# Inputs laid out on the host in the order of the loads, in a kernel of attention, dense gated layer and expert layer

## The chip, the cores and the metric

One core of one Trainium2 chip runs the whole program once. The metric is the device time of that core in microseconds, as the median of repeated executions; lower is better. The arrays that the kernel is given may be laid out on the host before the launch (a transposition or a reordering by numpy), and that takes no device time.

## The reference

Three layers follow each other, on 2304 tokens of width 512.

```python
scores = scale * np.matmul(q, k.transpose(0, 1, 3, 2))      # q, k, v: 4 x 8 x 576 x 64
ret = scores * Dmat[None, :, :, :]                          # gamma_h ** (i - j) for j <= i
x = np.matmul(ret, v)                                       # -> 2304 x 512

xn = x / rms * rms_g
g = xn @ w_gate                                             # 512 x 1536, float64
x = (g * sigmoid(g) * (xn @ w_val)) @ w_out                 # 1536 x 512, float64

e_idx = np.argmax(x @ w_gate2, axis=1)                      # one of 8 experts for a token
h = np.maximum(x[mask] @ w1[e], 0.0)                        # 512 x 1024
out[mask] = gate_w[mask, None] * eom[mask, e, None] * (h @ w2[e])
```

The weights of the dense layer are float64 on the device too: the kernel reads them as 64-bit integers and makes a high and a low float16 part of each. A product of two split numbers takes three matmuls (high by high, high by low, low by high).

## The kernel before, in words

The tokens are 18 tiles of 128 (`TILES`, L67), in groups (`GROUPS`, L70); group 0 holds tiles 0 to 3, one for each batch entry. For a tile, attention is loaded (`l`), split or transposed (`s`), scored (`c`), put out and normed (`o`), and its recurrent state updated (`z`). Then the dense layer runs over 12 slices of 128 hidden columns: `moe_h` (L828) makes a slice of the hidden activations, `moe_out` (L859) multiplies it by the output weights. At the end come routing and eight experts.

Group 0 is the opening. Its weights arrive in 18 pieces of 1 MB (`load_piece`, L806): piece i below 12 is gate and val of slice i, the other six are two slices of w_out each. `conv_piece` (L817) decodes a piece: `decode` (L784) puts a float64 together as a float32 (an operation on ScalarE, one on VectorE, and for each half a copy into the only PSUM buffer `du` and a VectorE operation out of it), ScalarE rounds it to `gv_h` or `wo_h`, and GpSimd subtracts for `gv_l` or `wo_l`. The raw pieces stand in `fst`, a pool of four buffers.

The first four tiles (`FIRST`, L76) need no state. Their q and k are loaded in rows of 64 numbers for each head (`att_load`, L586), and `split_first` (L603) transposes them on TensorE, eight transposes a tile, into PSUM tiles `tp`, from which ScalarE copies to `tr`. `scores_first` (L618) multiplies in float32, VectorE multiplies by the decay matrix `dmat` into `pp`, and `att_out` (L725) multiplies by v. Tile 2's loads borrow the buffer of tag `r` (`IN_R`).

The order of work is made by a planner (`Plan`, L236). Every operation is recorded with what it reads and writes, and `schedule` (L349) gives each engine a fixed list: at each planned moment an engine takes the ready operation with the lowest due time, which is the position of the first TensorE group that depends on it. A tile's buffers are taken in the recorded order (`_track`, L300), so an operation that first uses a buffer goes ahead of the one that first uses the next buffer of the same tag. `START` (L86) lists the opening's steps in the order in which they are recorded: `d` loads a piece, `k` decodes it, `f` makes `dmat` and `gain`, `h` is `moe_h`, `y` is `moe_out`, `e` clears a table in memory by GpSimd, `m` loads the router's weights. While TensorE has nothing to do in the plan and the first `y` hasn't begun, `fill` (L416) adds a matmul on a constant tile, `busy`, of 256 columns. All loads except those of tables are issued by SyncE (SP) on one queue. `_cost` (L322) has the planner's estimates.

Later tiles load q, k, v in the same short rows (L596). The experts' weights come in slabs of 1 MB (`exp_slab`, L1028) in rows of 2 KB.

Of the kernel before, what the change touches and what calls it, by code (L numbers as in the profile page):

```python
# [88 lines left out]
l4 o3 s4 y1-2-3 d7 k8 d14 k6 c4 d9 y1-0-1 k7 h3-4-3-4 k14 d15 h4-5-0-3 y3-1-2 y3-2-3 h0-2-3-4 k9 d11 e4 h6-7-3-4
h5-6-0-3 z3 d10 y2-0-3 l5 h7-8-0-3 z2 l6 y4-0-2 y5-0-3 d17 h5-6-3-4 k15 o4 z4 k10 m e2 s5 h2-3-3-4 y4-2-3 h6-7-0-3  # L90
y6-0-1 k11 y7-0-2 e8 h8-9-0-3 h4-5-3-4 h8-11-3-4 c5 y6-2-3 y7-2-3 d16 s6 h11-12-0-3 k16 e1 y6-1-2 e6 o5 c6 y8-0-3
k17 h9-11-0-3 o6 z6 e7 e5 y9-0-3 y10-0-1 y10-1-3 y11-0-3 e3 h7-8-3-4 z5 h11-12-3-4 e9
# [406 lines left out]
def body(tc, q, k, v, w_gate, w_val, w_out, rms_g, wg2, wog2, w1, w2, const, decay, empty, out):  # L499
# [169 lines left out]
    def att_scores(t):  # L669
# [358 lines left out]
    def exp_slab(slab, e, after=()):  # L1028
# [3 lines left out]
        def load():  # L1032
            w, at = (w1, slice(512 * slab, 512 * slab + 512)) if slab < 2 else (w2, slice(512 * slab - 1024, 512 * slab - 512))
            one = w[e] if isinstance(e, int) else w[bass.ds(e.result if isinstance(e, Op) else e, 1)].rearrange(
                "o d f -> (o d) f"
            )
            src = one[:, at] if slab < 2 else one[at, :]
            return nc.sync.dma_start(out=real(st), in_=src.rearrange("(k p) f -> p k f", p=P))
# [393 lines left out]
    def start():  # L1432

        for step in START.split():
# [173 lines left out]
```

## Time and profile before

| | us |
|---|---|
| median of 3 runs | 750.03 (749.82 to 750.12) |
| the profiled execution | 752.39 |
| its span | 750.6 |

| engine | busy, us | share of the span |
|---|---|---|
| TensorE, matmuls (PE) | 729.6 | 97% |
| TensorE, weight loads (PEld) | 495.2 | 66% |
| VectorE (DVE) | 432.9 | 58% |
| ScalarE (ACT) | 349.7 | 47% |
| GpSimd (POOL) | 282.1 | 38% |

The busy time of TensorE includes the matmuls on the constant tile. SP's instructions are DMA issues and count as no busy time. A row of the timeline gives start, length, engine, line, operation, output and inputs, and in brackets how long the engine was idle before it and what released it. The line is nearly always L226, the helper that records an operation, so that tile names tell operations apart. The DMA share of a stretch can be above 1, as packets of one engine overlap.

### The profile page before, as it was taken

To read this page: it belongs to the slowest core of one execution; us is meant where nothing else is said; L and a number is where in the kernel's file an instruction comes from. 1 tells how busy PE (TensorE), PEld (TensorE's weight loads), DVE (VectorE), ACT (ScalarE), POOL (GpSimd) and SP (SyncE) were. 2 spreads that over 40 slices of the span, in tenths; PEclk is the share of its full clock that TensorE was granted. 3 is DMA by queue.
4 is the path that set the end of the run, shared out by engine and by line. 5 is a ranking of instruction groups with operands and counts; after the bars stand their busy time and mean duration, and the time that the engine had idled before them with its cause. 6 is when DMAs were issued, how large, how long until landed. Compare 5 with 4: busy or idle time off the path is not lost. (4 is left out here: it accounts for less than half of the span.)

```text
span 750.6 us, 15489 instructions
## 1 busy us (share of the span) xinstructions
PE 729.6 (97%) x6163; PEld 495.2 (66%) x6163; DVE 432.9 (58%) x881; ACT 349.7 (47%) x665; POOL 282.1 (38%) x303
## 2 busy tenths in 40 slices
PE   9999999999899999999999999999999999999994
PEld 7986757656565656556655555677876677778751
DVE  3769898656662476157543626342565777666441
ACT  2789888533432264134422325222334666565450
POOL 2585789743541352215321311131103053313442
PEclk9999999999999999999999999999999999999998
DMA  9969989593670283435432143210089898899731
GB/s 237 255 195 240 271 195 266 116 203 62 132 146 18 61 164 74 73 43 117 82 57 43 58 108 132 43 58 15 15 253 263 258 290 220 264 268 238 186 98 38
DMA packets 212812, 109.84 MB, mean 146 GB/s; under 512 B 179891, under 2 KB 192211, under 8 KB 212594
## 3 DMA queue, kind: packets, MB, share of 16 engines
q1 hardware_dynamic: 209042, 96.30, 54.5%
q0 software_dynamic: 3696, 12.54, 5.2%
q8 instruction: 49, 0.80, 0.5%
q14 instruction: 25, 0.20, 0.1%
HBM read 70.02 MB, written 14.00 MB: 112 GB/s over the span
## 5 line engine op out<-in xcount | busy, mean ns | idle before, releaser
L226 PEld LDWEIGHTS <-gv_h 128*128 128x128 f16 x1440 | 133.3, 98 | 71.9 <-issue 6.0
L288 POOL TENSOR_TENSOR ul<-th,uh 128x384 f16<-128x384 f32 (+2 forms) x77 | 66.8, 868 | 209.1 <-ACT uh L226 207.9
L226 PE MATMUL hg<-xt,gv_h 128*128 128x384 f16 (+2 forms) x624 | 134.6, 305 | 1.9 <-DVE th L226 1.6
L226 PE MATMUL hv<-xt,gv_h 128*128 128x384 f16 (+2 forms) x624 | 135.9, 308 | 0.3 <-DVE th L226 0.3
L226 PEld LDWEIGHTS <-eh 128*128 128x128 f16 x1024 | 97.2, 98 | 30.0
L226 DVE SCALAR_TENSOR_TENSOR th<-th,hg 128x384 f32<-128x384 f32 (+2 forms) x90 | 42.3, 470 | 110.6 <-ACT th L226 110.5
L226 PE MATMUL eh<-ex,eh 128*128 128x288 f16 (+7 forms) x576 | 104.7, 284 | 0.0
L226 PE MATMUL hv<-xt,gv_l 128*128 128x384 f16 (+2 forms) x312 | 94.6, 307 | 0.0
L226 PE MATMUL hg<-xt,gv_l 128*128 128x384 f16 (+2 forms) x312 | 94.1, 305 | 0.0
L226 PEld LDWEIGHTS <-gv_l 128*128 128x128 f16 x720 | 70.6, 98 | 30.7 <-issue 0.7
L226 DVE SCALAR_TENSOR_TENSOR el<-st,eh 128x1024 f16<-128x1024 f32 x64 | 81.8, 1305 | 13.1 <-ACT eh L288 12.0
L226 ACT ACTIVATE uh<-th 128x384 f16<-128x384 f32 (+2 forms) x78 | 37.5, 481 | 97.3 <-DVE th L226 97.2
L226 ACT ACTIVATE th<-hg 128x384 f32<-128x384 f32 (+2 forms) x90 | 38.2, 424 | 93.2 <-PE hg L226 91.9
L226 PE MATMUL eh<-ex,el 128*128 128x288 f16 (+7 forms) x288 | 78.9, 284 | 0.0
L226 PE MATMUL o<-wo_h,ul 128*128 128x512 f16 x204 | 77.3, 379 | 0.0
L226 PE MATMUL o<-wo_h,uh 128*128 128x512 f16 x204 | 77.3, 379 | 0.0
L226 PE MATMUL o<-wo_l,uh 128*128 128x512 f16 x204 | 77.3, 379 | 0.0
L288 ACT ACTIVATE eh<-st 128x1024 f16<-128x1024 f32 x64 | 64.8, 1051 | 4.6 <-DMA st<-in_moe_w 4.6
L226 PE MATMUL ea<-hh,eh 128*128 128x288 f16 (+5 forms) x224 | 64.9, 290 | 0.0
L226 PE MATMUL ea<-hh,el 128*128 128x288 f16 (+5 forms) x224 | 64.9, 290 | 0.0
L226 PE MATMUL ea<-hl,eh 128*128 128x288 f16 (+5 forms) x224 | 64.9, 290 | 0.0
L226 DVE SCALAR_TENSOR_TENSOR th<-th,hv 128x384 f32<-128x384 f32 (+2 forms) x90 | 42.4, 471 | 32.1 <-PE hv L226 30.0
(210 smaller groups left out, 1223.3 us busy)
## 6 DMA issues: line engine op xcount, KB each, us to landing
st<-in_moe_w SPq DMA_DIRECT2D x32, 1024.0 KB
st<-in_moe_w_gate SPq DMA_DIRECT2D x12, 512.0 KB
st<-in_moe_w_val SPq DMA_DIRECT2D x12, 512.0 KB
st<-in_moe_w_out SPq DMA_DIRECT2D x12, 512.0 KB
kf<-in_k SPq DMA_DIRECT2D x15, 256.0 KB
qf<-in_q SPq DMA_DIRECT2D x15, 256.0 KB
vf<-in_v SPq DMA_DIRECT2D x15, 256.0 KB
xs<-in_empty POOLq DMA_DIRECT2D x7, 385.5 KB, 5.8
```

Of the source, the lines that this page charges most:

```text
L226: return call(*map(real, args), **{a: real(b) for a, b in kw.items()})
L288: return getattr(engine, method)(*map(real, args), **{a: real(b) for a, b in kw.items()})
```

## The change

The host transposes and reorders the inputs (`laid_out`), so that each load reads one long row for each partition: q, k and v of a token in rows of 2 KB, a piece of the dense weights in rows of 8 KB by one DMA, a slab of an expert in rows of 8 KB, the router's two tables in one load. For the first four tiles, q and k come transposed as one array `qk_t` (4 KB rows); the TensorE transposes and their copies go, k in rows is still loaded for the state, and q in rows no longer. The pool of raw pieces has five buffers for four, the score tile `pp` two for one; the scores of tiles 0 and 1 and the tables of step `f` use the PSUM pool `pso` in place of `pst`. The planner counts 330 GB/s for every plain load, also for those under 300 KB, and 3.3 us for a slab in place of 3.4. `START` is another list. The scratch for software-made DMA descriptors is set to 4096 bytes.

```diff
 START = """
-l0 d1 f l1 s0 c0 k1 d0 k0 s1 l2 o0 c1 o1 s2 h0-1-0-2 d12 d3 z0 c2 h1-2-0-1 d2 o2 d5 k3 h1-2-1-2 h3-4-0-2 k12
-h3-4-2-3 h0-1-2-3 l3 z1 y0-0-3 s3 c3 d13 k2 h1-2-2-3 d4 e0 h2-3-0-1 y1-1-2 k5 d8 k13 d6 h2-3-1-2 h2-3-2-3 y3-0-1 k4
...
+l2 l1 l0 s1 f d1 s0 s2 c0 o0 k1 d0 z0 d12 c1 d3 o1 k0 h0-1-0-2 d2 z1 k3 c2 h1-2-0-1 h1-2-1-2 o2 z2 h3-4-0-2 k12 d5
+h0-1-2-3 y0-0-1 k2 y0-2-3 h1-2-2-3 d13 l3 l4 d4 e0 h2-3-0-1 ...
...
-            rate = 174e3 if method == "dma_start_transpose" else 210e3 if size < 300e3 else 330e3
+            rate = 174e3 if method == "dma_start_transpose" else 330e3
...
-    fst = pool("fst", bufs=4)
+    fst = pool("fst", bufs=5)
...
     def att_load(t):
         tiles = []
-        own = at.tile([P, 3, H, 2, D], F16, tag="r", name=f"l{t}", bufs=2) if t == IN_R else None
-        for i, (nm, src) in enumerate((("k", k), ("q", q), ("v", v))):
-            if own is None:
-                a = at2.tile([P, H, D], F32, tag=nm + "f", name=f"{nm}f{t}")
+        if t in FIRST:
+            if t == IN_R:
+                both = at.tile([P, 3, H, 2, D], F16, tag="r", name=f"l{t}", bufs=2).rearrange("p a h c d -> p (a h c d)")
             else:
-                a = own[:, i].rearrange("p h c d -> p (h c d)").bitcast(F32).rearrange("p (h d) -> p h d", d=D)
+                both = at.tile([P, 3, H, P], F16, tag="tr", name=f"tr{t}", bufs=2).rearrange("p a h t -> p (a h t)")
+            both = both.bitcast(F32)[:, 0 : 2 * (H // 2) * P]
+            sy.dma_start(out=both, in_=qk_t[t])
+            tiles.append(both.rearrange("p (a b t) -> p a b t", a=2, b=H // 2))
+        for nm, tag, src in (("v", "v", v), ("k", "k", k)) if t in FIRST else (("k", "k", k), ("q", "q", q), ("v", "v", v)):
+            a = at2.tile([P, H, D], F32, tag=("q" if t == IN_R else tag) + "f", name=f"{nm}f{t}")
             o = 0
             for b, s0, n in TILES[t]:
-                sy.dma_start(out=a[o : o + n], in_=src[b, :, s0 : s0 + n, :].rearrange("h p d -> p h d"))
+                sy.dma_start(out=a[o : o + n].rearrange("p h d -> p (h d)"), in_=src[b * S + s0 : b * S + s0 + n])
...
     def split_first(t):
-        kf, qf, vf = qkv.pop(t)
-        tr = at.tile([P, 3, H, P], F16, tag="tr", name=f"tr{t}", bufs=2)
-        both = []
-        for i, src in enumerate((kf, qf)):
-            a = psh.tile([P, 4, P], F32, tag="h", name="tp")
-            with plan.group():
-                for b in range(4):
-                    te.transpose(a[:, b, :], src[:, 2 * b : 2 * b + 2].rearrange("p h d -> p (h d)"), identf)
-            dst = tr[:, i].rearrange("p h t -> p (h t)").bitcast(F32).rearrange("p (b t) -> p b t", t=P)
-            copy16("first", dst, a)
-            both.append(dst)
-        split[t] = kf, both, vf
+        both, vf, kf = qkv.pop(t)
+        split[t] = kf, (both[:, 0], both[:, 1]), vf
...
-        (kt, qt), p = split[t][1], at.tile([P, 2, H, P], F16, tag="pp", name=f"pp{t}")
+        (kt, qt), p = split[t][1], at.tile([P, 2, H, P], F16, tag="pp", name=f"pp{t}", bufs=PPB)
...
-            ps = pst.tile([P, 4, P], F32, tag="t", name=f"sc{t}_{g}")
+            pl, tag = (pso, "o") if t in IN_O else (pst, "t")
+            ps = pl.tile([P, 4, P], F32, tag=tag, name=f"sc{t}_{g}")
...
     def load_piece(i):
         raw[i] = st = fst.tile([P, 2, 512], I64, tag="st", name="st")
-        for j in range(2):
-            if i < NF:
-                src = (w_gate, w_val)[j][:, P * i : P * i + P]
-                sy.dma_start(
-                    out=st[:, j].rearrange("p (k f) -> p k f", f=P), in_=src.rearrange("(k p) f -> p k f", p=P)
-                )
-            else:
-                loads.append(sy.dma_start(out=st[:, j], in_=w_out[P * (2 * (i - NF) + j) : P * (2 * (i - NF) + j + 1), :]))
+        o = sy.dma_start(out=st.rearrange("p j f -> p (j f)"), in_=w_in[i])
+        if i >= NF:
+            loads.append(o)
...
+            one = w_exp[slab, i] if isinstance(i, int) else w_exp[slab, bass.ds(i, 1)].rearrange("o p f -> (o p) f")
+            return nc.sync.dma_start(out=real(st).rearrange("p k f -> p (k f)"), in_=one)
...
-        o = plan.op("SP", load, (), (st,), us=0.45, transfer=3.4, after=[e] if isinstance(e, Op) else ())
+        o = plan.op("SP", load, (), (st,), us=0.45, transfer=3.3, after=[e] if isinstance(e, Op) else ())
...
+        sy.dma_start(out=wgf.rearrange("p k e -> p (k e)"), in_=w_route)
...
-                a = pst.tile([P, DM], F32, tag="t", name="gb")
+                a = pso.tile([P, DM], F32, tag="o", name="gb")
...
+def laid_out(x):
+    x = {n: np.asarray(a) for n, a in x.items()}
+    q, k, v = (x[n].transpose(0, 2, 1, 3).reshape(NT, H * D) for n in "qkv")
+    first = np.stack([x[n][:, :, :P].reshape(B, H // 2, 2, P, D).transpose(0, 2, 4, 1, 3) for n in "kq"], axis=3)
+    gate, val = (x["moe_" + n].view(np.int64).reshape(KC, P, NF, P).transpose(2, 1, 0, 3) for n in ("w_gate", "w_val"))
+    rows = x["moe_w_out"].view(np.int64).reshape(NF // 2, 2, P, DM).transpose(0, 2, 1, 3)
+    w_in = np.concatenate([np.stack([gate, val], axis=2).reshape(NF, P, -1), rows.reshape(NF // 2, P, -1)])
...
-    nc = bacc.Bacc("TRN2", target_bir_lowering=False, num_devices=1)
+    nc = bacc.Bacc("TRN2", target_bir_lowering=False, num_devices=1, dynamic_dma_scratch_size=4096)
```

## Rows read from the trace of the kernel before

**Rows 1.** The page, its first part: busy time, share and instructions of the engines.

```profile
PE 729.6 (97%) x6163; PEld 495.2 (66%) x6163; DVE 432.9 (58%) x881; ACT 349.7 (47%) x665; POOL 282.1 (38%) x303
```

**Rows 2.** Windows, expert phase: length, busy time by engine, granted clock, DMA share, GB/s.

```profile
600.00:700.00 100.00, 100.00 (x802) 78.31 (x801) 66.14 (x101) 58.91 (x110) 32.65 (x33) 1.00 0.95 251
```

**Rows 3.** The tile `busy`: its matmuls' duration, first and last start.

```profile
L226 PE MATMUL busy<-warm x165: 272/273/421, 1.0 to 49.8; 128*128 128x256 f16 x165
```

**Rows 4.** Timeline of TensorE in the opening: start, length, operation, count.

```profile
1.05 4.39 PE L226 MATMUL busy<-warm 128*128 128x256 f16 x23 [1.05 <-DVE warm L226]
...
37.12 0.39 PE L226 MATMUL hg<-xt,gv_h 128*128 128x256 f16 x2
...
42.75 2.46 PE L226 MATMUL busy<-warm 128*128 128x256 f16 x21
...
50.54 0.38 PE L226 MATMUL o<-wo_h,uh 128*128 128x512 f16 x1
...
53.83 0.60 PE L226 MATMUL tp<-identf,kf 128*128 128x128 f32 x4
...
55.11 0.27 PE L226 MATMUL hg<-xt,gv_h 128*128 128x128 f16 x2 [0.25 <-ACT tr L288]
```

**Rows 5.** Waits of TensorE from 50 us on: total, times, longest.

```profile
PE hg L226 <- DVE th L226: 3.1, 3, 1.6
```

**Rows 6.** Windows with one kind of load in flight, columns as in rows 2.

```profile
7.00:9.50 2.50, 2.50 (x15) 1.56 (x13) 0.00 (x0) 1.19 (x2) 0.00 (x0) 1.00 1.35 219
11.00:12.00 1.00, 1.00 (x12) 1.00 (x11) 0.61 (x2) 0.00 (x0) 0.00 (x0) 1.00 1.09 343
...
113.50:117.00 3.50, 3.50 (x60) 3.26 (x59) 2.69 (x8) 3.39 (x9) 3.50 (x3) 1.00 1.02 415
```

**Rows 7.** Timeline of VectorE: the first operation that needs a load.

```profile
3.78 0.29 DVE L226 TENSOR_TENSOR identf<-cst 128x128 f32<-128x128 f32 x1 [1.32 <-DMA cst<-in_const]
```

**Rows 8.** Timeline of ScalarE: the start of the first piece's decode.

```profile
18.72 0.60 ACT L288 ACTIVATE xt<-tp 128x512 f16<-128x512 f32 x1 [2.59 <-PE tp L226]
19.21 1.13 ACT L226 ACTIVATE st<-st 128x1024 int32<-128x1024 uint32 x1
```

**Rows 9.** Timeline of GpSimd: the low half of piece 0.

```profile
33.19 2.13 POOL L288 TENSOR_TENSOR gv_l<-st,gv_h 128x1024 f16<-128x1024 f32 x1 [2.93 <-ACT gv_h L288]
```

**Rows 10.** The tile `st`: least, median and greatest duration of the decode's operations, in ns.

```profile
L288 ACT ACTIVATE du<-st x36: 623/642/686, 20.2 to 133.5; 128x512 f32<-128x512 f32 x36
L226 DVE SCALAR_TENSOR_TENSOR st<-du,st x36: 673/686/698, 21.9 to 134.2; 128x512 int32<-128x512 int32 x36
...
L226 ACT ACTIVATE st<-st x18: 1127/1177/1217, 19.2 to 121.1; 128x1024 int32<-128x1024 uint32 x18
L226 DVE SCALAR_TENSOR_TENSOR st<-st x18: 1214/1304/2704, 20.6 to 128.2; 128x1024 int32<-128x1024 int32 x18
...
L288 ACT ACTIVATE gv_h<-st x12: 1127/1152/1184, 26.6 to 117.8; 128x1024 f16<-128x1024 f32 x12
L288 POOL TENSOR_TENSOR gv_l<-st,gv_h x12: 2115/2156/2344, 28.1 to 119.0; 128x1024 f16<-128x1024 f32 x12
```

**Rows 11.** Timeline of VectorE in group 1: one stretched operation.

```profile
185.61 5.59 DVE L226 SCALAR_TENSOR_TENSOR r<-qf,r 128x512 f16<-128x512 f32 x1
```

**Rows 12.** Timeline of TensorE in group 1: its longest wait.

```profile
191.92 0.69 PE L226 MATMUL sc<-tr 128*128 128x128 f16 x8 [2.52 <-DVE xh L226]
```

**Rows 13.** Windows behind that wait, columns as in rows 2.

```profile
190.00:195.00 5.00, 3.08 (x17) 1.69 (x17) 4.82 (x7) 2.20 (x4) 1.70 (x2) 0.73 0.79 156
```

**Rows 14.** Windows, from the first decode to the last one's end.

```profile
19.00:136.00 117.00, 113.26 (x1197) 87.64 (x1196) 98.57 (x155) 96.70 (x174) 86.92 (x74) 1.00 0.91 239
```

**Rows 15.** The page: packets of GpSimd's queue, and its clears with time to landing.

```profile
q0 software_dynamic: 3696, 12.54, 5.2%
...
xs<-in_empty POOLq DMA_DIRECT2D x7, 385.5 KB, 5.8
```

**Rows 16.** Timeline of GpSimd: the first of eight clears up to 135.7 us.

```profile
123.64 1.07 POOL L1384 DMA_DIRECT2D xs<-in_empty  x2
```

More of the change, by code (lines that the diff above doesn't have):

```diff
@@ L79 @@
 VSB = 2
+PPB = 2
+IN_O = (0, 1)
 X0 = 4
@@ L86 @@
 START = """
-l0 d1 f l1 s0 c0 k1 d0 k0 s1 l2 o0 c1 o1 s2 h0-1-0-2 d12 d3 z0 c2 h1-2-0-1 d2 o2 d5 k3 h1-2-1-2 h3-4-0-2 k12
-h3-4-2-3 h0-1-2-3 l3 z1 y0-0-3 s3 c3 d13 k2 h1-2-2-3 d4 e0 h2-3-0-1 y1-1-2 k5 d8 k13 d6 h2-3-1-2 h2-3-2-3 y3-0-1 k4
[L89 to L92, printed above, removed]
+l2 l1 l0 s1 f d1 s0 s2 c0 o0 k1 d0 z0 d12 c1 d3 o1 k0 h0-1-0-2 d2 z1 k3 c2 h1-2-0-1 h1-2-1-2 o2 z2 h3-4-0-2 k12 d5
+h0-1-2-3 y0-0-1 k2 y0-2-3 h1-2-2-3 d13 l3 l4 d4 e0 h3-4-2-3 k5 y0-1-2 s4 d8 s3 k13 d6 d7 y1-2-3 c3 h2-3-0-1 y3-0-1
+o3 y1-0-2 d14 h2-3-1-3 e3 m k4 y3-2-3 k8 d9 y2-0-3 d15 e8 y3-1-2 h3-4-3-4 h0-1-3-4 h4-6-0-3 k6 k7 c4 e1 k14 h6-7-3-4
+h8-9-0-3 k15 z3 o4 y4-1-2 y4-2-3 l5 y4-0-1 h2-3-3-4 z4 k9 h1-2-3-4 d10 y5-0-1 e4 k10 d11 y5-1-3 d16 h7-8-3-4
+h7-8-0-3 h6-7-0-3 y7-1-2 y7-2-3 h5-6-3-4 k16 k11 e5 s5 y6-0-1 d17 l6 h4-5-3-4 y6-1-3 y7-0-1 s6 c5 c6 k17 o5 y8-0-3
+o6 h9-12-0-3 y9-0-3 e6 e2 e9 h8-10-3-4 y10-0-3 z6 e7 y11-0-3 z5 h10-12-3-4
 """
@@ L496, in decays, with body @@
     return d.astype(np.float32)
-def body(tc, q, k, v, w_gate, w_val, w_out, rms_g, wg2, wog2, w1, w2, const, decay, empty, out):
+def body(tc, q, k, v, qk_t, w_in, rms_g, w_route, w_exp, const, decay, empty, out):
     nc = tc.nc
@@ L673, in att_scores @@
         m = C_MASK if len(TILES[t]) == 1 else C_MASKP
-        p = at.tile([P, 2, H, P], F16, tag="pp", name=f"pp{t}")
+        p = at.tile([P, 2, H, P], F16, tag="pp", name=f"pp{t}", bufs=PPB)
         ph, pl = p[:, 0], p[:, 1]
@@ L1032, in load @@
         def load():
[L1033 to L1038, printed above, removed]
-        o = plan.op("SP", load, (), (st,), us=0.45, transfer=3.4, after=[e] if isinstance(e, Op) else ())
+            i = e if isinstance(e, int) else e.result if isinstance(e, Op) else e
+            one = w_exp[slab, i] if isinstance(i, int) else w_exp[slab, bass.ds(i, 1)].rearrange("o p f -> (o p) f")
+            return nc.sync.dma_start(out=real(st).rearrange("p k f -> p (k f)"), in_=one)
+        o = plan.op("SP", load, (), (st,), us=0.45, transfer=3.3, after=[e] if isinstance(e, Op) else ())
         if after:
@@ L1422, in router_consts @@
     def router_consts():
-        sy.dma_start(out=wgf[:, :, 0:E], in_=wg2.rearrange("(k p) e -> p k e", p=P))
-        sy.dma_start(out=wgf[:, :, E : 2 * E], in_=wog2.rearrange("(k p) e -> p k e", p=P))
+        sy.dma_start(out=wgf.rearrange("p k e -> p (k e)"), in_=w_route)
         ve.memset(ones, 1.0)
@@ L1442, in start @@
                 sy.dma_start(out=gain[0:1], in_=rms_g.unsqueeze(0))
-                rise = at.tile([P, 2, H, P], F16, tag="pp", name="rise").rearrange("p a h t -> p (a h t)").bitcast(F32)
+                rise = at.tile([P, 2, H, P], F16, tag="pp", name="rise", bufs=PPB).rearrange("p a h t -> p (a h t)").bitcast(F32)
                 ve.memset(rise, 0.0)
@@ L1457, in start @@
                 for i in range(2):
-                    a = pst.tile([P, 4, P], F32, tag="t", name="db")
+                    a = pso.tile([P, 4, P], F32, tag="o", name="db")
                     te.matmul(
@@ L1576, in body @@
         pl.release()
-_INS = ["q", "k", "v", "moe_w_gate", "moe_w_val", "moe_w_out", "moe_rms_g",
-        "moe2_w_gate", "moe2_w_output_gate", "moe2_w1", "moe2_w2"]
+def laid_out(x):
+    import numpy as np
+    x = {n: np.asarray(a) for n, a in x.items()}
[4 more added lines that the diff above has]
+    w_in = np.concatenate([np.stack([gate, val], axis=2).reshape(NF, P, -1), rows.reshape(NF // 2, P, -1)])
+    route = [x["moe2_" + n].reshape(KC, P, E).transpose(1, 0, 2) for n in ("w_gate", "w_output_gate")]
+    w1 = x["moe2_w1"].reshape(E, KC, P, 2, 512).transpose(3, 0, 2, 1, 4).reshape(2, E, P, KC * 512)
+    w2 = x["moe2_w2"].reshape(E, 2, KC, P, DM).transpose(1, 0, 3, 2, 4).reshape(2, E, P, KC * DM)
+    return {
+        "q": q, "k": k, "v": v, "qk_t": first.reshape(B, P, -1), "w_in": w_in, "rms_g": x["moe_rms_g"],
+        "w_route": np.concatenate(route, axis=2).reshape(P, -1), "w_exp": np.concatenate([w1, w2]),
+    }
 def kernel(**inputs):
@@ L1586 @@
     from concourse.bass_utils import run_bass_kernel_spmd
-    nc = bacc.Bacc("TRN2", target_bir_lowering=False, num_devices=1)
+    nc = bacc.Bacc("TRN2", target_bir_lowering=False, num_devices=1, dynamic_dma_scratch_size=4096)
     arrays, args = {}, []
-    for name in _INS:
-        a = np.ascontiguousarray(inputs[name])
-        if a.dtype == np.float64:
-            a = a.view(np.int64)
+    for name, a in laid_out(inputs).items():
+        a = np.ascontiguousarray(a)
         arrays[f"in_{name}"] = a
```

## The prediction

> **What bounds the kernel now.** The page's busy table comes first: TensorE is busy for 729.6 us of a 750.6 us span [rows 1], and in the expert phase for all of 100 us [rows 2]. Nothing that the change does to loads or tables there can be worth time: expert slabs with 8 KB rows, the 3.3 for 3.4 in their planned transfer and the single router load cost and give nothing, because the rows behind them show no idle TensorE to fill.
>
> The busy share is deceptive in the opening. The group `busy` is 165 matmuls on a constant tile, put in by the planner wherever it finds TensorE without work before the first `y` step [rows 3]. The first 23 take 4.39 us from 1.05 on; the other 142 take (2.46 - 0.27) / 20 = 0.109 us each, by the run of 21 at 42.75 whose last one's 0.27 is taken off, 15.5 us. With the first 1.05 us, some 20.9 of the first 50.5 us are no work. The first matmul on decoded weights (`hg`, step h0) starts at 37.12, the first `y` at 50.54 [rows 4]. From there to the end TensorE's waits, without its tail, add up to 9.1 us; 3.5 of them, nearly all in the group of `hg` waiting for VectorE's `th` [rows 5], lie before 110 us. So the end is set by when h0 starts, by the TensorE work from there on, and by what is lost after it. Note that the fillers are instructions in a fixed order: they can't be skipped when data come early, and between 1.05 and 55.11 us TensorE never idled [rows 4]; the chip kept pace with the plan.
>
> **What decides h0.** It needs piece 0 of the weights decoded. Three rates of the DMA engines can be read where one kind of row is in flight: q, k and v with 256 B rows at 219 GB/s, gate and val with 1 KB rows at 343, w_out with 4 KB rows (some transposes and 256 B rows among them) at 415 [rows 6]. The constants, issued first at 0.73, released VectorE at 3.78 [rows 7]; 0.27 MB at 343 GB/s is 0.8 us, so some 3.0 us from the span's start are first issue and landing, once.
>
> Before, ahead of the end of piece 1 (loaded first) stand 2.10 MB of q, k, v, 1.05 MB of weights, 0.31 MB of constants: 9.6 + 3.1 + 0.9 + 3.0 = 16.6 us. ScalarE took it at 19.21, after waiting 2.59 us for transposes of `tp` on TensorE [rows 8]; the piece lay ready meanwhile. The low half of piece 0, the last thing that h0 needs, began at 33.19 and lasts 2.13 [rows 9]. So from landing to h0 there are 20.5 us, more than the loads themselves.
>
> The bare decode is shorter. By the medians [rows 10]: 1.18 (ACT) + 1.30 (DVE) + 2 x (0.64 + 0.69) for the two halves through the only `du` buffer = 5.1; piece 0's two halves behind it 2.7; then 1.15 (ACT) and 2.16 (POOL): 11.1 us for the two pieces. From ScalarE's start to 35.32 it took 16.1, so 5.0 us were spent on attention work between, on engines that run in order.
>
> **The change, part by part.**
>
> Loads. The transposed q and k of a first tile are 0.52 MB on top of rows of k and v (q in rows is dropped): 1.05 MB a tile in place of 0.79. START begins with l2 l1 l0, and a buffer's earlier user is issued first, so all three transposed pairs (1.57 MB), v and k of two tiles (1.05) and constants (0.31) go ahead of the weights, then pieces 1 and 0. Up to the end of piece 1 that is 3.98 MB: 9.6 us at 415 GB/s, 11.6 at 343, plus 3.0: it lands at 12.6 to 14.6, I take 13.6. The new rows are 2 to 8 KB, and the nearest row is the 4 KB one, but the small constants are in the sum, hence the middle. Two issues of SP become one for each weight piece, and one queue of SP carries fewer commands; SP was not what was late.
>
> By the Trainium skill ("DMA: Bandwidth & Descriptors", Specifications) HBM gives one core about 358 GB/s; its section on measured bandwidth adds that this is with both cores of a domain streaming. Here one core streams and the row shows 415, so the row decides; at 358 the piece would land at 14.1, which moves the forecast by 0.5 us.
>
> Transposes. Eight TensorE transposes a tile and two ScalarE copies go. For the first three tiles they lie in time that fillers fill, so on TensorE they are worth nothing; on ScalarE two copies of 0.60 sat in the decode's 16.1 us, so 3.8 of the 5.0 us between stay (0 to 5.0 as bounds). For the fourth tile they lie behind the first `y`: from the first of two groups at 53.83 to the next `hg` at 55.11, a wait of 0.25 us on their copy included [rows 4]: 1.3 us of the path.
>
> Buffers. A second `pp`, scores of tiles 0 and 1 in pso, a fifth weight buffer: they add no instruction, they let a tile's scores go on while the former tile's are in use. The pso buffers are wanted by `y` accumulators only later, and their earlier users end before. I count this inside the 3.8 us, at nothing of its own. `dynamic_dma_scratch_size=4096` pays for it in memory (a rival below).
>
> Order. h0 at 13.6 + 11.1 + 3.8 = 28.5 us, for 37.1: gain 8.6. Bounds: 12.6 + 11.1 = 23.7 and 14.6 + 16.1 = 30.7, gains 13.4 and 6.4. TensorE has 36.1 - 16.2 (fillers until then) - 3.1 (six groups of transposes, by the two in 53.83 to 54.86) = 16.8 us of work to do before 28.5, so it is not what is late. What is late next is the decode: 18 pieces, of which two are ready at h0, as before. The 3.7 us of fillers after 37.12 (34 of them, the longest run in [rows 4]) and the 3.5 us of idle up to 110 I leave as they are: from 7.2 less (better supply, five buffers) to 3.9 more. The latter is one stall such as at 191.92, where a VectorE operation stretched to 5.59 us held TensorE for 2.52 us, after which the granted clock of 190 to 195 us was 0.73, some of it at the lower level of 1.2 GHz: (1 - 0.73) x 5 = 1.4 us of work more [rows 11 to 13]. Any shift of the opening can add or remove one.
>
> Sum: 8.6 + 1.3 = 9.9 us. The profiled execution took 752.39 us, span 750.6; it becomes 742.5. The median of the timed runs is 750.03, 2.36 below the profiled one, so the prediction is 740.1 us; with the bounds of this case 728 to 746, its ends needing all terms at once.
>
> **The rivals.**
> - Decode is the pace (746): from 19 to 136 us VectorE is busy 98.57 and ScalarE 96.70 of 117 [rows 14]. VectorE loses no work by the change. If it can't be packed more tightly, the whole train only shifts with piece 1's landing, 16.6 to 13.6, and 1.3 comes off TensorE: 4.3 less. Against it: 18 us of slack in those 117, and waits for transposes that go.
> - Supply catches up (733): the later fillers and idle vanish too, 9.9 + 7.2 less. For it: faster loads and the fifth buffer; against it: the same ScalarE and VectorE work for each piece.
> - Slower (752.5): long rows bring no rate where SBUF is written for the first tiles, and the extra megabyte stands ahead of the weights. At 219 GB/s for q, k, v piece 1 lands at 12.0 + 3.1 + 0.9 + 3.0 = 19.0, 2.4 later; with the old 20.5 us behind it h0 is at 39.5. The planner, which counts 330 GB/s for every load in the changed code, has laid too few fillers for that, so TensorE idles and restarts at the low clock, 1.4 us by [rows 13]: 2.4 + 1.4 - 1.3 = 2.5 more. It decides once piece 1 lands after 17.7. Against it: 343 and 415 are seen with rows that are longer.
> - The smaller scratch holds POOL's own transfers back (757): eight clears are issued by POOL within 12 us from 123.64 on [rows 16], with the last `wo_l` among them; their landing takes 5.8 us [rows 15]. If each waited for the one before, 12 us became 46, of which the later consumers would hide half: some 17 us more, less the 9.9 gained. It decides where a ring holds less than two clears. Against it: that queue moves only 3696 packets in the whole run [rows 15]. The Trainium skill ("SBUF — State Buffer", SBUF size) calls this scratch the software queue's descriptor ring, 16 KiB by default; no row here shows it full.
> - It doesn't do what it says (750): the planner fills the time gained at the start with fillers later, because decode order, not loads, stands behind it.
>
> **How the numbers follow.** Forecast 0.55, supply catches up 0.10, decode is the pace 0.19, no net change 0.05, slower by late loads 0.08, slower by POOL 0.03. A measurement of this kernel can tell about 0.2% (1.5 us) from no change. Faster: 0.55 + 0.10 + 0.19 = 0.84; same 0.05; slower 0.11. The range from 731.5 to 748 holds the forecast with all but the far ends of its bounds and both of the faster rivals, and leaves out the last three.
>
> **What would show it.** Right: first `hg` at 24 to 31 us; 165 `busy` matmuls become some 80 to 90; DMA above 340 GB/s from 3 to 15 us; no `tp` from kf, qf or l; first `y` near 41; the busy work after it unchanged. Wrong: TensorE idle for a DMA between 5 and 30 us (late loads); h0 early but idle or fillers after it (decode); waits of POOL's queue on its own transfers; another stretched VectorE operation in 180 to 400 us.

## The result, and the profile after

The changed kernel takes 742.17 us (median of 4 runs, 741.01 to 742.64) where the kernel before takes 750.07 (749.82 to 750.12) beside it: ratio 0.9893 [0.9876, 0.991], 7.9 us less. A second set of runs gave 742.97, beside 749.71 before, and 0.9906 [0.9887, 0.9925]. The profiled execution took 741.83 us, with a span of 740.0 us and a granted clock of 0.998; before it was 752.39, 750.6 and 0.994. Line numbers move: the recording helper is L228 now, the copies are L290.

The page after, its head, first part and third part (beside [rows 1] and [rows 15]):

```profile
span 740.0 us, 15260 instructions
PE 723.5 (98%) x6080; PEld 488.7 (66%) x6080; DVE 438.7 (59%) x878; ACT 345.8 (47%) x655; POOL 281.1 (38%) x303
...
DMA packets 139418, 110.87 MB, mean 150 GB/s; under 512 B 123395, under 2 KB 123427, under 8 KB 132802
```

TensorE is busy for 6.1 us less, and the packets fall from 212812 to 139418. The timeline of TensorE in the opening, after (beside [rows 4]):

```profile
1.04 7.37 PE L228 MATMUL busy<-warm 128*128 128x256 f16 x41 [1.04 <-DVE warm L228]
8.25 1.02 PE L228 MATMUL gb<-gain,cst 128*128 128x512 f32 x2
...
9.22 1.88 PE L228 MATMUL db<-rise,fall 128*128 128x512 f32 x4
11.04 3.09 PE L228 MATMUL sc<-tr 64*128 64x128 f32 x24
14.06 2.00 PE L228 MATMUL pa<-vf,pp 128*128 128x64 f32 x16
...
31.54 3.77 PE L228 MATMUL busy<-warm 128*128 128x256 f16 x33
35.14 0.38 PE L228 MATMUL hg<-xt,gv_h 128*128 128x256 f16 x2
35.50 0.28 PE L228 MATMUL hg<-xt,gv_l 128*128 128x256 f16 x1
...
44.16 0.82 PE L228 MATMUL busy<-warm 128*128 128x256 f16 x6
...
48.30 0.38 PE L228 MATMUL busy<-warm 128*128 128x256 f16 x2
48.52 0.38 PE L228 MATMUL o<-wo_h,uh 128*128 128x512 f16 x1
```

The first `hg` starts at 35.14, for 37.12 before: 2.0 us earlier, not 8.6. There are 138 fillers for 165, and only 8 of them lie behind the first `hg`, for 34.

Windows of the opening, after: length, busy time by engine, granted clock, DMA share, GB/s.

```profile
5.00:10.00 5.00, 5.00 (x29) 3.23 (x28) 0.00 (x0) 1.88 (x2) 0.00 (x0) 1.00 1.02 364
10.00:15.00 5.00, 5.00 (x35) 4.00 (x35) 3.46 (x5) 0.00 (x0) 0.00 (x0) 1.00 0.98 363
...
20.00:25.00 5.00, 5.00 (x53) 4.45 (x53) 4.51 (x7) 3.71 (x8) 2.72 (x3) 1.00 1.02 425
```

The loads run as fast as predicted, at 364 and 363 GB/s where the kernel before shows 206 and 265 in the same windows. ScalarE and GpSimd in the opening, after (beside [rows 8, 9]):

```profile
7.96 1.28 ACT L228 ACT_TABLE_LOAD   x1 [7.96 <-DMA gain<-in_rms_g]
...
16.09 0.60 ACT L228 ACTIVATE junk<-pa 128x512 f16<-128x512 f32 x1 [6.18 <-PE pa L228]
16.59 0.20 ACT L228 ACTIVATION_READ_ACCUMULATOR junk<-pa 128x1 f32 x1
16.68 1.14 ACT L228 ACTIVATE st<-st 128x1024 int32<-128x1024 uint32 x1
19.45 0.60 ACT L290 ACTIVATE xt<-tp 128x512 f16<-128x512 f32 x1 [1.63 <-PE tp L228]
19.94 0.62 ACT L290 ACTIVATE zh<-z 128x512 f16<-128x512 f32 x1
...
26.84 0.60 ACT L290 ACTIVATE xt<-tp 128x512 f16<-128x512 f32 x1 [0.58 <-PE tp L228]
...
29.96 0.63 ACT L290 ACTIVATE zh<-z 128x512 f16<-128x512 f32 x1
...
30.67 1.68 POOL L290 TENSOR_TENSOR zl<-z,zh 128x512 f16<-128x512 f32 x1 [2.72 <-ACT zh L290]
32.31 3.13 POOL L290 TENSOR_TENSOR gv_l<-st,gv_h 128x1024 f16<-128x1024 f32 x1
```

Here `pa` is a tile's attention output, `junk` its squares for the norm, `xh` and `xt` the normed tile and its transpose, `zh` and `zl` the halves of the recurrent state. ScalarE takes the first weight piece at 16.68, right behind `junk`, which had waited for the first attention tile (`pa`). The last thing that h0 needs, the low half of piece 0, ends at 35.44. Its first matmul starts at 35.50.

Before, that half ended at 33.19 + 2.13 = 35.32 [rows 9]. So ScalarE starts 2.5 us earlier on the weights, and the piece is ready no earlier. The 2.0 us at the first `hg` are TensorE's: before, its fixed order came to `hg` 1.8 us after the half was ready (37.12), now it comes just as the half gets ready. ScalarE's other work between, before:

```profile
25.18 0.62 ACT L288 ACTIVATE zh<-z 128x512 f16<-128x512 f32 x1
26.12 0.60 ACT L288 ACTIVATE xt<-tp 128x512 f16<-128x512 f32 x1 [0.32 <-PE tp L226]
...
27.65 0.59 ACT L288 ACTIVATE tr<-tp 128x512 f32<-128x512 f32 x1
...
30.31 0.60 ACT L288 ACTIVATE tr<-tp 128x512 f32<-128x512 f32 x1
```

The longer stretch behind h0 is read from two windows, each from the first `hg` to the first `rt` (ScalarE's first copy of a finished dense output `o`). Before:

```profile
37.10:144.60 107.50, 103.76 (x1128) 76.66 (x1127) 88.46 (x146) 86.99 (x160) 85.02 (x76) 1.00 0.85 219
```

After:

```profile
35.10:139.90 104.80, 101.01 (x1058) 72.76 (x1057) 87.14 (x141) 82.87 (x152) 83.32 (x73) 1.00 0.75 211
```

TensorE idles 3.7 us in the one and 3.8 in the other; the 2.7 us between them are busy time. The 26 fillers fewer are 2.8 us by the prediction's 0.109 us each, and the fourth tile's transposes were 1.0 us of busy time; some 1.1 us of other work between these two marks, which I haven't followed further, eat up part of it. At the first `rt` the changed kernel is 4.7 us ahead (139.9 for 144.6).

The end of the program holds a gain that no line of the diff on an engine explains. GpSimd's last scatter, before and then after:

```profile
741.75 0.98 POOL L1186 DMA_INDIRECT out<-y,yx  x1 [3.84 <-DVEq L1572]
```

```profile
733.68 0.98 POOL L1175 DMA_INDIRECT out<-y,yx  x1 [3.84 <-DVEq L1560]
```

From its start to the end of the span it is 750.6 - 741.75 = 8.85 us before and 740.0 - 733.68 = 6.3 us after: 2.5 us.

What is left of the 10.6 us between the two spans, 3.4 us, lies from 140 to 521 us. About 1.8 of it is the granted clock of one stretch, which differs between executions of the same kernel. The same 20 us, after and then the second profile of the same kernel:

```profile
180.00:200.00 20.00, 17.47 (x163) 10.71 (x162) 16.63 (x22) 11.52 (x25) 12.57 (x14) 1.00 0.62 150
```

```profile
180.00:200.00 20.00, 17.47 (x156) 10.52 (x154) 15.32 (x20) 10.36 (x22) 12.04 (x13) 0.91 0.56 136
```

In both, TensorE had waited 2.5 us for the tile `xh`, as in [rows 12]; before, the clock of these 20 us was 0.91 too. In the second profile, with its span of 741.9, the four parts are 2.2 (to the first `hg`), 2.8 (to the first `rt`), 1.2 (to the last `o`) and 2.5 (the end).

### The profile page after: what moved, and what is told of

Same layout as the page of the kernel before. It is cut to its first block, busy times and chain, and to the rows that moved or that the text cites. A ratio compares the mean times of both kernels' runs of the same rounds, so it can differ in the third digit from the quotient of the medians.

```text
span 740.0 us, 15260 instructions
## 1 busy us (share of the span) xinstructions
PE 723.5 (98%) x6080; PEld 488.7 (66%) x6080; DVE 438.7 (59%) x878; ACT 345.8 (47%) x655; POOL 281.1 (38%) x303
## 5 line engine op out<-in xcount | busy, mean ns | idle before, releaser
L228 PEld LDWEIGHTS <-gv_h 128*128 128x128 f16 x1424 | 131.8, 98 | 70.5 <-issue 3.7
L290 POOL TENSOR_TENSOR ul<-th,uh 128x384 f16<-128x384 f32 (+2 forms) x77 | 68.4, 889 | 213.9 <-ACT uh L228 213.5
L228 PE MATMUL hv<-xt,gv_h 128*128 128x384 f16 (+2 forms) x616 | 134.4, 308 | 1.2 <-DVE th L228 1.2
L228 PE MATMUL hg<-xt,gv_h 128*128 128x384 f16 (+2 forms) x616 | 134.5, 308 | 0.6 <-DVE th L228 0.6
L228 PEld LDWEIGHTS <-eh 128*128 128x128 f16 x1024 | 97.1, 98 | 30.1
L228 DVE SCALAR_TENSOR_TENSOR th<-th,hg 128x384 f32<-128x384 f32 (+2 forms) x89 | 42.2, 474 | 116.0 <-ACT th L228 116.0
L228 PE MATMUL eh<-ex,eh 128*128 128x288 f16 (+7 forms) x576 | 104.7, 284 | 0.0
L228 PE MATMUL hg<-xt,gv_l 128*128 128x384 f16 (+2 forms) x308 | 93.8, 308 | 0.0
L228 PE MATMUL hv<-xt,gv_l 128*128 128x384 f16 (+2 forms) x308 | 93.8, 308 | 0.0
L228 DVE SCALAR_TENSOR_TENSOR el<-st,eh 128x1024 f16<-128x1024 f32 x64 | 84.7, 1353 | 11.7 <-ACT eh L290 11.3
L228 PEld LDWEIGHTS <-gv_l 128*128 128x128 f16 x712 | 69.5, 98 | 30.7 <-POOL gv_l L290 0.3
L228 ACT ACTIVATE th<-hg 128x384 f32<-128x384 f32 (+2 forms) x89 | 38.0, 427 | 99.9 <-PE hg L228 97.7
L228 ACT ACTIVATE uh<-th 128x384 f16<-128x384 f32 (+2 forms) x77 | 37.2, 483 | 93.9 <-DVE th L228 93.8
L228 PE MATMUL eh<-ex,el 128*128 128x288 f16 (+7 forms) x288 | 79.0, 284 | 0.0
L228 PE MATMUL o<-wo_h,uh 128*128 128x512 f16 x204 | 77.4, 379 | 0.0
L228 PE MATMUL o<-wo_l,uh 128*128 128x512 f16 x204 | 77.4, 379 | 0.0
L228 PE MATMUL o<-wo_h,ul 128*128 128x512 f16 x204 | 77.4, 379 | 0.0
L290 ACT ACTIVATE eh<-st 128x1024 f16<-128x1024 f32 x64 | 64.7, 1050 | 3.4 <-DMA st<-in_w_exp 3.3
L228 PE MATMUL ea<-hh,eh 128*128 128x288 f16 (+5 forms) x224 | 65.0, 290 | 0.0
L228 PE MATMUL ea<-hh,el 128*128 128x288 f16 (+5 forms) x224 | 65.0, 290 | 0.0
L228 PE MATMUL ea<-hl,eh 128*128 128x288 f16 (+5 forms) x224 | 65.0, 290 | 0.0
L228 PEld LDWEIGHTS <-uh 128*128 128x128 f16 x408 | 38.4, 98 | 34.7
```

What stands on the lines that cost most here:

```text
L228: return call(*map(real, args), **{a: real(b) for a, b in kw.items()})
L290: return getattr(engine, method)(*map(real, args), **{a: real(b) for a, b in kw.items()})
```

## Experiments: one part alone, or all but one

The first set asked which part carries the gain: the rows, the list, the transposes, or which weight piece comes first. The planner ran again in each of them, so each has another instruction order. In the same runs the kernel before took 752.87 us (751.28 to 753.31).

**rows_alone**, the long rows in the kernel before, with its list, buffers, rates and scratch:

```diff
-                sy.dma_start(out=a[o : o + n], in_=src[b, :, s0 : s0 + n, :].rearrange("h p d -> p h d"))
+                sy.dma_start(out=a[o : o + n].rearrange("p h d -> p (h d)"), in_=src[b * S + s0 : b * S + s0 + n])
...
+        o = sy.dma_start(out=st.rearrange("p j f -> p (j f)"), in_=w_in[i])
```

> The kernel before with the host layout's long rows alone: q and k of the first tiles still in rows and transposed on TensorE, old list, old buffers, old planner rates, old scratch. Theory A (faster loads carry the gain): piece 1 lands some 2 us earlier, first hg near 35, 745 to 747 us. Theory B (the list and its buffers carry it; loads in themselves were no limit): first hg stays at 36.5 to 37.1 because the order and the number of fillers are fixed by the planner, 749 to 750.5 us.

**old_list**, the changed kernel with the list of before (its `z2` moved ahead of `l4`):

```diff
-l2 l1 l0 s1 f d1 s0 s2 c0 o0 k1 d0 z0 d12 c1 d3 o1 k0 h0-1-0-2 ...
+l0 d1 f l1 s0 c0 k1 d0 k0 s1 l2 o0 c1 o1 s2 h0-1-0-2 d12 d3 z0 ...
```

> The changed kernel with the START list of before (step z2 moved ahead of l4, which its buffers ask for), all else as changed. Theory A: 742 to 744.5 us, most of the gain stays. Theory B: 746 to 750 us, most of it goes with the list.

**pe_transposes**, the changed kernel without the transposed array: q and k in rows and the TensorE transposes of before (`s2` moved ahead of `c2`).

```diff
-            sy.dma_start(out=both, in_=qk_t[t])
...
+                    te.transpose(a[:, b, :], src[:, 2 * b : 2 * b + 2].rearrange("p h d -> p (h d)"), identf)
```

> The changed kernel without the transposed array: q and k of the first tiles come in long rows and are transposed on TensorE (s2 moved to just before c2), new list, buffers and rates. By the prediction's step, only the fourth tile's transposes lie on the path: 1.3 us more, 0 to 1 us less for 1 MB fewer bytes ahead of the weights: 742.5 to 743.5 us. Rival: the copies and transposes of the first three tiles delay the decode on ScalarE, first hg 2 to 4 us later than 35.1: 745 to 747 us.

**piece0_first**, the changed kernel with weight piece 0 loaded and decoded ahead of piece 1:

```diff
-l2 l1 l0 s1 f d1 s0 s2 c0 o0 k1 d0 z0 d12 c1 d3 o1 k0 h0-1-0-2 ...
+l2 l1 l0 s1 f d0 s0 s2 c0 o0 k0 d1 z0 d12 c1 d3 o1 k1 h0-1-0-2 ...
```

> The changed kernel with pieces 0 and 1 exchanged in load and decode (d0, k0 ahead of d1, k1). If the decode of piece 0, last in its queue, sets the first hg, it starts 2.5 to 4 us earlier, at 31 to 32.5; if the time of the first hg then sets the end: 739 to 740.5 us. Rival (the whole train of decodes sets the end, whatever comes first): first hg earlier, but more fillers or waits after it, 741.5 to 743 us.

Measured, in the order of the ratios: rows_alone 758.68 us, 1.0092 [1.0065, 1.0119]; old_list 757.45, 1.0059 [1.0046, 1.0072]; pe_transposes 756.76, 1.0052 [1.004, 1.0065]; piece0_first 756.42, 1.0045 [1.0032, 1.0057]. All four are slower than the kernel before, though three of them hold most of the change, and none of the times named beforehand came, by either theory. The marks of the traces say how:

| kernel | first `hg` | first `rt` | between |
|---|---|---|---|
| before | 37.12 | 144.63 | 107.5 |
| after | 35.14 | 139.85 | 104.7 |
| rows_alone | 38.96 | 151.80 | 112.8 |
| pe_transposes | 33.49 | 149.89 | 116.4 |
| old_list | 32.61 | 152.04 | 119.4 |
| piece0_first | 29.28 | 151.98 | 122.7 |

piece0_first starts h0 within the 24 to 31 us that the prediction asked for, 7.8 us earlier than before, and reaches the first `rt` 7.4 us later. The time gained at h0 is lost behind it. Waits of TensorE in piece0_first from 29 to 145 us (total, times, longest):

```profile
PE tp L228 <- DVE th L228: 3.5, 1, 3.5
PE hg L228 <- DVE th L228: 3.4, 2, 3.2
PE hg L228 <- POOL gv_l L290: 2.6, 2, 1.4
PE hv L228 <- DVE th L228: 2.1, 2, 1.5
```

The same view of old_list:

```profile
PE hg L229 <- DVE th L229: 11.4, 7, 3.8
```

And what such waits do to the clock, windows of old_list:

```profile
80.00:90.00 10.00, 5.34 (x68) 4.62 (x67) 9.11 (x17) 9.48 (x19) 9.98 (x10) 0.90 0.76 271
90.00:100.00 10.00, 6.25 (x33) 3.56 (x32) 8.08 (x8) 5.41 (x10) 6.86 (x7) 0.75 1.06 284
```

TensorE is busy 5.34 of 10 us while VectorE (9.11), ScalarE (9.48) and GpSimd (9.98) are full. So an early h0 is worth something only if these three can feed what follows; that depends on the whole order, and each of these four kernels got another one. They therefore don't price the parts. They show that the parts don't add up, and that h0 is not the mark that sets the end.

## Experiments: the order held still

In the second set, on a chip where the kernel before took 749.71 us (748.95 to 750.68), the planner's view of each load was kept, so that every engine has the same instructions in the same order as its parent. Only the rows of the DMAs differ.

**after_again**, the changed kernel itself, is given above.

> The changed kernel itself, beside the three below on the same chip. 741 to 745 us, about 1.1% under the kernel before; a second trace shows which of its waits recur.

**short_rows**, the changed kernel's order with short rows: 256 B for q, k, v and the transposed array, 2 KB for the slabs, and 1 KB for all weight pieces (before, gate and val had 1 KB, w_out 4 KB).

```diff
-            sy.dma_start(out=both, in_=qk_t[t])
+            sy.dma_start(out=both.rearrange("p (a d) -> p a d", d=D), in_=qk_t[t].rearrange("a p d -> p a d"))
...
-        o = sy.dma_start(out=st.rearrange("p j f -> p (j f)"), in_=w_in[i])
+        o = sy.dma_start(out=st.rearrange("p j (k f) -> p (j k) f", f=P), in_=w_in[i].rearrange("a p f -> p a f"))
```

> The changed kernel with every engine's instructions in the same order, but q, k, v in HBM as before (256 B rows), the transposed pairs in 256 B rows, weight pieces in 1 KB rows, slabs in 2 KB rows. Theory C (a fixed order: what the loads bring is worth time only where TensorE would wait for them): by the rates at 219 and 343 GB/s piece 1 lands at 19 to 20 in place of 14 and the decode behind it shifts; the order was made for early loads, so TensorE idles before the first hg, 39 to 41 us, and the run takes 747 to 751 us. Rival (the loads have slack, the gain is the order's alone): 742 to 744.5 us.

Measured: 747.66 us, 0.9974 [0.9965, 0.9983]. Beside after_again (742.97) the long rows are worth 4.7 us in this order; what w_out's share of that is, whose rows are shorter here than they ever were, no run separates. The time is the one of theory C. The first `hg` comes at 36.42, earlier than the 39 to 41 us expected, and TensorE then waits for what it found ready in the changed kernel. At the first `rt` short_rows is at 143.9, for 139.6 in after_again. Timeline of TensorE in short_rows, then of ScalarE at its first weight piece:

```profile
38.22 0.28 PE L228 MATMUL hg<-xt,gv_l 128*128 128x256 f16 x1 [1.41 <-POOL gv_l L290]
```

```profile
19.12 1.15 ACT L228 ACTIVATE st<-st 128x1024 int32<-128x1024 uint32 x1 [1.54 <-DMA st<-in_w_in]
```

Up to 140 us ScalarE waits nine times for the load of a weight piece, 11.9 us in all. In the changed kernel these waits are absent from the first profile and 0.8 us in the second: there the loads don't hold the decode, with short rows they do.

**long_rows**, the kernel before in its own order, with the long rows and as many DMAs as it had:

```diff
-                src = (w_gate, w_val)[j][:, P * i : P * i + P]
...
+            o = sy.dma_start(out=st[:, j], in_=w_in[i][:, 512 * j : 512 * j + 512])
```

> The kernel before with every engine's instructions in the same order and the same number of DMAs, only each DMA's rows in HBM made long (2 KB for q, k, v, 4 KB for half a piece, 8 KB for a slab). Theory C: TensorE never waited for a load before 50 us, its 165 fillers stand in the order, so earlier data can't be used: first hg at 37.0 to 37.2, 165 fillers, and the time within 0.4% of before. Rival (loads as such are worth the gain): first hg at 34 to 35, 3 to 6 us less.

Measured: 751.01 us, 1.0013 [1.0004, 1.0022]. The loads are fast and nothing comes of it. A window and the first `hg` of long_rows:

```profile
10.00:15.00 5.00, 5.00 (x33) 3.64 (x33) 2.77 (x4) 0.73 (x2) 0.00 (x0) 1.00 1.00 396
```

```profile
1.04 5.09 PE L226 MATMUL busy<-warm 128*128 128x256 f16 x23 [1.04 <-DVE warm L226]
...
38.12 0.39 PE L226 MATMUL hg<-xt,gv_h 128*128 128x256 f16 x2
```

396 GB/s in that window for 265 before, the same 165 fillers, and `hg` at 38.12, later than before by the 0.7 us that the first 23 fillers took longer in this execution (5.09 for 4.39) and some 0.3 more. The fillers and the order don't know that the data came early.

**later_short**, the changed kernel with short rows of q, k and v from the fifth tile on:

```diff
+                if t in FIRST:
+                    sy.dma_start(out=a[o : o + n].rearrange("p h d -> p (h d)"), in_=src[b * S + s0 : b * S + s0 + n])
+                else:
+                    sy.dma_start(out=a[o : o + n], in_=short[nm][b, :, s0 : s0 + n, :].rearrange("h p d -> p h d"))
```

> The changed kernel with the same order, only q, k, v of the tiles from the fifth on in 256 B rows as before. If the 3.4 us gained behind the first group (waits of sc for VectorE that got shorter) come from these loads: 1.5 to 3.5 us more. Rival (they come from where VectorE and GpSimd happen to meet): within 1 us of the changed kernel.

Measured: 741.32 us, 0.9893 [0.9879, 0.9908], the same as the changed kernel within the noise, as the rival had it. So the 4.7 us come from the other loads, those of the first tiles and of the weights; which of these, no run separates.

## Experiments: the end, the fillers, the tables

The third set, with the kernel before at 750.01 us (749.18 to 751.09).

**small_scratch**, the kernel before, its order untouched:

```diff
-    nc = bacc.Bacc("TRN2", target_bir_lowering=False, num_devices=1)
+    nc = bacc.Bacc("TRN2", target_bir_lowering=False, num_devices=1, dynamic_dma_scratch_size=4096)
```

> The kernel before with the smaller dynamic DMA scratch (4096) and nothing else; every engine's instruction order is that of before. It asks for the 2.5 us by which the stretch from the last expert matmul to the span's end is shorter in the changed kernel (8.4 us for 10.9), which no line of the change that touches an engine explains. Theory (the end of the program depends on the scratch): last expert matmul at about 740 as before, span end 8.4 us behind it, 2.5 us faster: about 747.5 for 750.0, ratio 0.997. Rival (the short end comes from the number of inputs or of instructions): tail 10.9 us, ratio 1.000. Rival of the prediction (POOL's queue held back): slower, with waits of POOL's transfers around 123 to 136 us.

Measured: 748.06 us, 0.9973 [0.9961, 0.9985], 2.0 us faster, with a span of 746.2 us. GpSimd's last scatter in small_scratch:

```profile
739.84 0.98 POOL L1186 DMA_INDIRECT out<-y,yx  x1 [3.84 <-DVEq L1572]
```

From there to the span's end it is 6.4 us. The kernels with the scratch of before show 8.8 to 8.9 (before, long_rows, rows_alone), all those with the small one 6.3 to 6.4. So the one argument that the prediction held for a pure risk is a gain of about 2 us, and the shorter end is its work. By the same numbers the new order with short rows (short_rows, 0.9974) is worth no more than the scratch that it contains (0.9973), as far as two ratios good to 0.1% tell: **the new order, with its buffers and without the transposes, gives nothing of its own until the loads are fast, and fast loads give nothing without it.** Which of the three (order, buffers, absent transposes) the fast loads need, no run separates.

**fewer_late**, the changed kernel without 26 of the 33 fillers ahead of the first `hg`:

```diff
+CUT = range(104, 130)
...
+                n += o.idx < 0
+                if o.idx < 0 and n in CUT:
+                    continue
```

> The changed kernel with 26 of the 33 filler matmuls ahead of the first hg left out, every other instruction in its place. Theory (the decode holds h0: the low half of piece 0 is ready at 35.44 and its first matmul starts at 35.50): the first matmul on gv_l stays at 35 to 35.5, TensorE shows about 2.8 us of waiting for gv_h or gv_l instead of fillers; the time is the same within 0.2%, or up to 1.5 us longer where the clock falls after the wait. Rival (TensorE's fixed sequence holds h0): first hg and all behind it 2.8 us earlier, ratio 0.986 to 0.987 for 0.990.

Measured: 744.52 us, 0.9926 [0.9913, 0.9938], some 2 us slower than the changed kernel. Timeline of TensorE in fewer_late, and the windows around its wait:

```profile
31.68 0.38 PE L230 MATMUL hg<-xt,gv_h 128*128 128x256 f16 x2
34.88 0.28 PE L230 MATMUL hg<-xt,gv_l 128*128 128x256 f16 x1 [2.81 <-POOL gv_l L292]
35.00 0.59 PE L230 MATMUL hg<-xt,gv_h 128*128 128x256 f16 x2
```

```profile
31.60:34.80 3.20, 0.46 (x5) 0.17 (x2) 3.11 (x4) 2.54 (x5) 3.20 (x3) 1.00 0.69 257
34.80:38.50 3.70, 3.62 (x18) 2.64 (x19) 2.82 (x4) 1.39 (x2) 2.52 (x3) 0.54 0.75 241
```

The matmul on `gv_l` hardly moves (34.88, for 35.50 and 35.24 in the two profiles of the changed kernel): it waits 2.81 us for GpSimd in place of the fillers, so at h0 the decode is the pace, not TensorE's sequence. And the fillers earn their place: after the wait the granted clock is 0.54 for 3.7 us, mostly the level of 1.2 GHz, and a pair of matmuls takes 0.59 us for 0.38; in the changed kernel the clock of the same stretch is 1.00. (1 - 0.54) x 3.7 = 1.7 us, near what this kernel lost; the expectation had up to 1.5. The match isn't exact: at the first `rt` this profile is only 0.6 and 0.9 us behind the two of the changed kernel (140.5 for 139.9 and 139.6), and its clock from 180 to 200 us is 0.91, as in the second of them.

**tables_early**, the changed kernel with the loads of the gain and decay tables moved up on SP's queue, and 18 of the first 41 fillers out:

```diff
+        at = order.index(self.cst) + 1
+        order[at:at] = [mg, g, mf, f]
+        at = order.index(self.tr) + 1
+        order[at:at] = [mr, r]
```

> The changed kernel with the three small loads of the gain and decay tables moved ahead of the transposed loads on SP's queue (gain and fall behind the constants, rise behind the first transposed load), and 18 of the first 41 fillers left out to make room; every other instruction in its place. In the changed kernel the gain table lands at 7.9 us, the gain and decay matmuls follow at 8.25, the first attention tile ends at 16.0, and ScalarE takes weight piece 1 at 16.68 though it has landed by about 14. Theory (the tables behind the transposed loads cost what the predicted h0 missed at its start): tables' matmuls at 5 to 6 us, the first attention tile 2.5 us earlier, ScalarE takes piece 1 at 14 to 14.5, first hg at 32 to 33.5 if nothing else holds it, time 2 to 2.7 us below the changed kernel: ratio 0.986 to 0.987. Rival (the loads or the decode's later steps hold h0): first hg stays at 34.5 to 35.5, ratio 0.989 to 0.991. Rival (clock): fewer fillers leave TensorE colder and the first attention tile is slower, ratio above 0.991.

Measured: 744.33 us, 0.9926 [0.9913, 0.9939]. The first `hg` stayed, as the rival had it, but for a reason of the experiment's own making. Timeline of TensorE in tables_early:

```profile
5.21 1.02 PE L230 MATMUL gb<-gain,cst 128*128 128x512 f32 x2
6.07 0.27 PE L230 MATMUL busy<-warm 128*128 128x256 f16 x1
9.36 1.95 PE L230 MATMUL db<-rise,fall 128*128 128x512 f32 x4 [3.02 <-DMA rise<-in_decay]
...
35.35 0.38 PE L230 MATMUL hg<-xt,gv_h 128*128 128x256 f16 x2
```

The gain table's matmul is 3.0 us earlier, as meant. But the large table `rise` was put behind the load of tile 2, which is issued last of the three transposed ones; so its issue went from 2.82 to 3.31 us, and TensorE waited 3.02 us for it. All behind it stands where it stood (`hg` 35.35). The ratio is the one that the rival of the clock asked for (above 0.991), but the first attention tile isn't slower here (`sc` x24 takes 3.09 us as in the changed kernel). The two profiles don't explain why the time came out above the changed kernel: the granted clock from 180 to 200 us was low here (0.91), and that differs between executions anyway. What `rise` ahead of the transposed loads would give wasn't tried.

**both**, the two together:

```diff
+CUT = [*range(20, 38), *range(104, 130)]
```

> Tables early and 26 of the 33 later fillers out, together. If the tables' late landing and the fixed fillers each hold h0, this is the one that shows the whole gain: first hg near 30 to 31, ratio 0.982 to 0.985. If the decode holds h0 alone, it comes out like tables_early. If the clock suffers from the idle time, it is slower than tables_early by 0.5 to 1.5 us.

Measured: 747.03 us (743.35 to 748.01), 0.9943 [0.9923, 0.9963]. It waits for `rise` (3.12 us) and for `gv_l` (2.83 us) as its two parts do, and is no faster than either alone; the gain that it was meant to show isn't there. No kernel here beats the changed one; later_short equals it.

## Why the prediction was right, and where it was not

The time was forecast at 740.1 us, range 731.5 to 748, and is 742.17. The sum was 9.9 us and the measured gain is 7.9. **The total is near, but by other terms than those named.** That it came near is luck: of the 8.6 us named for h0 2.0 came, while the later fillers (2.8) and the end of the program (2.0 to 2.5), both held at nothing, made up for much of the rest.

- **Loads** were right: 360 GB/s and more from 5 to 25 us. Piece 1 is among the two pieces issued from 8.15 us; with the median of 6.1 us from issue to landing of the weights' loads that is some 14.3 us, an estimate that agrees with 12.6 to 14.6. The window from 20 to 25 us shows 425 GB/s. The Trainium skill ("HBM Reference", Specifications (TRN2)) gives about 425 for a core that streams alone, beside the share of about 358 that the prediction weighed; the trace agrees with the former.
- **h0 = 13.6 + 11.1 + 3.8 = 28.5** was wrong: it is 35.1. Two terms were mis-sized. ScalarE started at 16.7, not at the landing: the order puts the first attention tile ahead, and that stands behind 41 fillers (up to 8.25) and the tables issued behind two transposed loads (`gain` released ScalarE's first instruction at 7.96; in after_again TensorE waited 0.36 us for it, up to 7.83). And from ScalarE's start to the end of `gv_l` it is 18.8 us, so 7.7 us beside the decode's 11.1, not 3.8. The prediction took off the two copies, and they went; but the new order puts an `xt` and a `zh` more in their place, so ScalarE's other work up to the end of `gv_h` is 3.2 us as before, and it idles 3.5 us for 2.5. On GpSimd `gv_l` then stands 0.7 us behind `zl` and takes 3.13 us for 2.13 in [rows 9]. So the stretch grew from 16.1 to 18.8 us, beyond the upper bound, and took back all of the earlier start.
- **"The end is set by when h0 starts"** was the step under it, and the table of marks contradicts it: piece0_first has h0 at 29.3 and is slower than before. From h0 to the first `rt` VectorE, ScalarE and GpSimd must feed 18 pieces and the attention; an early h0 without that supply becomes waits and low clock. Measured at the first `rt`, the gain is 4.7 us, near the 4.3 of the rival in which the decode is the pace, and not near 9.9. That rival's picture (the whole train shifts by the little that the start gains) was the better one, though not the whole: 2.0 of the 4.7 are there at h0, 2.7 come behind it.
- **Transposes** at 1.3: none of `kf`, `qf` or `l` is left on TensorE; 1.0 us of busy time went in the stretch of the two windows. No run priced them by themselves, since pe_transposes got another order.
- **Later fillers and idle** "as they are" (7.2 us in all): the fillers behind h0 fell from 34 to 8, 2.8 us, inside the bound given; the idle time stayed, 3.8 for 3.7.
- **Scratch**: taken as a risk of 17 us with a chance of 0.03 and never as a gain; it gave 2.0 us. The clears' median time to landing was 4.1 us after and 4.5 in small_scratch, for 5.8 in [rows 15]: nothing is held back.
- **Expert phase**: no gain, as said. From 600 to 700 us TensorE is busy for 100.00 us again, as in [rows 2].
- The median's 7.9 us are thus some 4.7 by the first `rt` and 2.0 to 2.5 at the end; the remaining 0.7 to 1.2 lie between, where the clock of single stretches varies from execution to execution and no run separates the parts.

Of what the prediction said would show it: the load rates and the absent transposes came; first `hg` at 24 to 31, 80 to 90 fillers and the first `y` at 41 didn't (35.1, 138, 48.5). By its own list of signs the reasoning was wrong on the opening, while the time fell near the forecast.

## What to carry to other kernels

In this kernel faster loads were worth nothing to a fixed order that was laid out for slow ones, and the new order little without them: change both, and test each with the order held still, since a planner that runs again changes everything at once. An early start of the bound engine is a gain only as far as the engines that feed it can follow, so put the mark at the end of the stretch that they feed, not at its beginning. And read the last microseconds too: a setting that no engine's timeline shows can be there.

## What the runs showed of the hardware

- The size of the dynamic DMA scratch sets how long the program takes to end behind its last scatter: 8.8 to 8.9 us by default (3 profiles), 6.3 to 6.4 with 4096 bytes (11 profiles), whatever the order and the inputs.
- The first fillers, on a TensorE that has just started, differ from execution to execution: 41 of them took 7.37, 6.43 and 6.21 us in after, after_again and later_short, which start alike, 23 took 4.39 and 5.09 in before and long_rows. All that is queued behind them shifts along: the first `hg` of later_short is at 34.04, 1.1 us ahead of 35.14.
- The clock's answer to a wait is no fixed price: 2.81 us of waiting ahead of 34.88 us was followed by 0.54; the 2.5 us ahead of 188 us by a clock of 1.00 from 180 to 200 us in one profile of the changed kernel and 0.91 in the other; 3.02 us ahead of 9.36 us in tables_early by no fall that the rows show (`sc` x24 took 3.09 us there as in the changed kernel).
